# Idle matmuls on the outputs' bank, bias rows loaded by threes, and more rounds of the order planner, in an attention and channel-mix kernel

## The chip, the cores and the metric

The kernel runs on one core of a Trainium2 chip. The metric is the device time of one execution in microseconds, and the time given for a kernel is the median of its runs.

The engines are named as the profile names them: PE multiplies matrices (PEld is its weight load, which runs beside the matmuls), DVE, ACT and POOL work element by element, and SP issues all DMAs of this kernel, from one queue and in order.

## The reference

There are 8 batches, 8 heads, 576 positions and a head dimension of 64. The model width is 512 and the hidden width 1024.

```python
scores = scale * q @ k.T                              # per batch and head
cum = np.cumsum(np.maximum(s, 0.0), axis=-1)
bias = -(cum[:, :, :, None] - cum[:, :, None, :])
scores = np.where(causal, -1e9, scores + np.minimum(bias, 0.0))
attn = softmax(scores)
x = concat_heads(attn @ v)                            # [batch, position, 512]

xk = mu_k * x + (1 - mu_k) * x_prev                   # x_prev: one position earlier
xr = mu_r * x + (1 - mu_r) * x_prev
k = np.maximum(xk @ w_k, 0.0)
v = k * k @ w_v
out = sigmoid(xr @ w_r) * v
```

The matrices of the second part (w_k, w_r, w_v) arrive as 64-bit floats.

## The kernel before, in words

**Attention.** Heads are visited in pairs. The first batch is visited twice: first the early tiles (queries and keys 0 to 319, called A) of its four pairs, then the late ones (Z). The other batches are visited once, with all 576 positions. For each head `scores` makes the products into a PSUM bank "s" (there are two; L687 in the first visits, L698 afterwards). DVE reads them (L715), adds the bias row or the masked bias, keeps the running minimum nm and writes W. ACT makes the exponentials (L733) and POOL divides by the sums (L749). In `weighted` PE turns the weights over (L795), ACT and DVE copy them (L822, L857), PE multiplies them with the values into the one bank "po" (L913 in the first visits, L927 afterwards), and ACT copies that out (L948, L955). POOL makes the masked bias from the bias row with a select (L669). The bias row of a head, 128 copies of its cumulative sums, is loaded from cum_d in DRAM (L650) into one of two buffers "cb"; heads 0 and 1 of the first batch compute theirs (L475). cum_d itself is written once at the start (L457).

**Channel mix.** The results of a pair go to DRAM (L1277) and come back by chunks of 256 positions (L1178). There are 18 chunks. Each mixes neighbouring positions (ACT L1025, then DVE L1032), splits the result in two parts (L1054, L1058), and multiplies with w_k (L1086), w_r (L1128) and w_v (L1153) in three products each. Every block of a weight is loaded (L504), turned from 64-bit to two 32-bit parts by one ACT (L527), four DVE (L532 to L550), one ACT (L556) and one POOL instruction (L558), and stays in SBUF. The space of w_v blocks 4 to 7 holds the first batch's early results until those blocks are loaded.

**The order.** Nothing is issued in the order of the code. Every instruction is a task with an engine, a planned duration, the tasks it depends on and a due time. `Plan.forward` runs a list schedule over the engines with planned costs (TAIL and GAPS are what a result needs to reach another engine). `Plan.backward` makes new due times from that schedule. `Plan.run` does PASSES rounds of both and emits the order with the shortest planned time. While PE has nothing ready within 170 ns and the first split products (L698) have not been reached, `forward` puts in idle matmuls: 192 columns of an identity, planned at 82 ns each, which compute nothing that is used. They are not tasks, so the planner sees no dependence between them and others; the framework that emits the instructions adds semaphores by the tiles they touch.

The idle matmuls of the kernel before write columns 320 to 511 of one of the two "s" banks:

```python
idle = bank(1, "s", 2)
plan.idle = lambda: nc.tensor.matmul(
    idle.get()[:, 320:512], ...
```

Of the kernel before, what the change touches and what calls it, by code (L numbers as in the profile page):

```python
# [14 lines left out]
BF16 = mybir.dt.bfloat16  # L15
# [38 lines left out]
class Plan:  # L54
# [225 lines left out]
        return [-x for x in at]  # L280


    PASSES = 8

    def run(self):
        best = None
# [14 lines left out]
def forgetting_attention_then_channel_mix(  # L301
# [15 lines left out]
    nc = tc.nc  # L317

    B, H, D, S = q.shape
    DM, DF = moe_w_k.shape  # L320
    P = 128
# [16 lines left out]
    plan = Plan()  # L338

    def sbuf(shape, tag, bufs=1, dtype=F32):  # L340
        return plan.buffer(sb, shape, dtype, tag, bufs)

    def bank(n, tag, bufs=1):
        return plan.buffer(psum, [P, 512 * n], F32, tag, bufs)
# [28 lines left out]
    def dma(emit, reads, writes, ns):  # L373
        return plan.add("SP", max(500, 1.2 * ns), emit, reads, writes, land=1500)


    ident = fixed(const.tile([P, P], F32, name="ident"))
    make_identity(nc, ident.ap)


    idle = bank(1, "s", 2)
    plan.idle = lambda: nc.tensor.matmul(  # L382
        idle.get()[:, 320:512],
        ident.ap.bitcast(BF16)[:, 0:P],
        ident.ap.bitcast(BF16)[:, 0:192],
        start=True,
        stop=True,
    )
    QS = [0] + [64 + P * t for t in range(NQ - 1)]
    QN = [64] + [P] * (NQ - 1)  # L390
    KN = [QS[t] + QN[t] for t in range(NQ)]
# [40 lines left out]
    cum_d = fixed(dram.tile([B * H, S], F32, name="cum_d"))  # L432
# [132 lines left out]
    ALL, A, Z = tuple(range(NQ)), (0, 1, 2), (3, 4)  # L565
    first = []
# [78 lines left out]
    def scores(b, h, tiles, G, KH, KL):  # L645

        NK = KN[tiles[-1]]
        CB = sbuf([P, NK], "cb", 2) if not first else first.pop(0)
        (b == 0 and h < 2 and tiles == A) or dma(
            lambda: nc.sync.dma_start(  # L650
                CB.get(), cum_d.ap[b * H + h : b * H + h + 1, 0:NK].broadcast_to([P, NK])
            ),
            [cum_d], [CB], 819 * NK / S,
        )
        nm, sums, rinv = (sbuf([P, n], x, 2) for x, n in (("nm", 3 * NQ), ("sums", NQ), ("rinv", NQ)))
        if 0 in tiles:
            pool(lambda: nc.gpsimd.memset(sums.get()[:, 0:1], 1.0), [], [(sums, 0)], 1, 160)
        pt = early[h % 4] if tiles == A else weights[h % 2]


        M = sbuf([P, S], "mask", 2)

        def mask(m, k0, n):
            def own(x):
                x = x.get()[:m, k0 : k0 + n * m]
                return x if n == 1 else x.rearrange("p (t x) -> p t x", x=m)

            pool(
                lambda: nc.gpsimd.affine_select(  # L669
                    out=own(M),  # L670
                    in_=own(CB),
                    pattern=[[-1, m]] if n == 1 else [[0, n], [-1, m]],
                    base=0,
                    channel_multiplier=1,
                    compare_op=ALU.is_ge,
                    fill=MASK * ISCALE,
                ),
                [CB], [(M, k0 > 0)], n * m, 137,
            )

        def products(t, m, i, k0, w, W):
            ps = bank(1, "s", 2)
            q0 = QS[t] - QS[tiles[0]]
            if KL is None:
                r = slice(64 * (h % 2), 64 * (h % 2) + 64)
                pe(
                    lambda: nc.tensor.matmul(  # L687
                        ps.get()[:m, :w],
                        G.get()[r, q0 : q0 + m],
                        KH.get()[r, k0 : k0 + w],  # L690
                        start=True,
                        stop=True,
                    ),
                    [(G, x) for x in range(2)] + [(KH, x) for x in range(2)], [ps], w + 80, m, 4 / 2.4, 64,
                )
            for x, K in enumerate((KH, KL) if KL is not None else ()):
                y = pe(
                    lambda x=x, K=K: nc.tensor.matmul(  # L698
                        ps.get()[:m, :w],
                        G.get()[:, q0 : q0 + m],  # L700
                        K.get()[:, k0 : k0 + w],
                        start=x == 0,
                        stop=x == 1,
                    ),
                    [(G, x) for x in range(2)] + [(K, x) for x in range(2)], [ps], w, m,
                )
                if plan.busy_from is None:
                    plan.busy_from = y

            for a, e in ((k0, min(k0 + w, QS[t])), (max(k0, QS[t]), k0 + w)):  # L710
                if a >= e:
                    continue
                bias = CB if a < QS[t] else M
                dve(
                    lambda a=a, e=e, bias=bias, i=i: nc.vector.tensor_tensor_reduce(  # L715
                        out=W.ap[:m, a:e],
                        in0=ps.get()[:m, a - k0 : e - k0],
                        in1=bias.get()[:m, a:e],
                        scale=-SCALE,
                        scalar=3.0e38 if i == 0 else nm.get()[:m, 3 * t + i - 1 : 3 * t + i],  # L720
                        op0=ALU.add,
                        op1=ALU.min,
                        accum_out=nm.get()[:m, 3 * t + i : 3 * t + i + 1],
                    ),
                    [ps, (bias, 0 if bias is CB else t > 0)] + ([(nm, (t, i - 1))] if i else []),
                    [(W, i), (nm, (t, i))], e - a, extra=143 if i else 78,
                )
                i += 1
            return i

        def exponents(t, m, n, mi, W):
            act(
                lambda: nc.scalar.activation(  # L733
                    W.ap[:m, :n],
                    W.ap[:m, :n],
                    AF.Exp,
                    bias=nm.get()[:m, 3 * t + mi : 3 * t + mi + 1],
                    scale=-1.0,
                    accum_out=sums.get()[:m, t : t + 1],
                ),  # L740
                [(nm, (t, mi))], [(W, i) for i in range(3)] + [(sums, t)], n, 290, 1,
            )

        def normalize(t, m, n, W):


            to, c = (pt[1], P) if t == 0 else (W, 0)
            pool(
                lambda: nc.gpsimd.tensor_scalar(  # L749
                    out=to.ap[:m, c : c + n],  # L750
                    in0=W.ap[:m, :n],
                    scalar1=rinv.get()[:m, t : t + 1],
                    scalar2=1.0,
                    op0=ALU.mult,
                    op1=ALU.mult,
                ),
                [rinv] + [(W, i) for i in range(3)], [(to, i) for i in range(3)], n, 244,
            )

        def rs(x):  # L760
            return x.get()[:, tiles[0] : tiles[-1] + 1]

        if 0 in tiles:
            mask(64, 0, 1)
        mask(P, QS[max(1, tiles[0])], len([t for t in tiles if t]))
        for t in tiles:
            m, n, W = QN[t], KN[t], pt[t]
            i = 0
            for k0, w in [(0, n)] if n <= 512 else [(0, n // 2), (n // 2, n // 2)]:
                i = products(t, m, i, k0, w, W)  # L770
            exponents(t, m, n, i - 1, W)
        pool(
            lambda: nc.gpsimd.tensor_scalar(
                out=rs(rinv), in0=rs(sums), scalar1=1.0e-9, scalar2=None, op0=ALU.add
            ),
            [(sums, t) for t in tiles], [rinv], len(tiles), 310,
        )
        dve(lambda: nc.vector.reciprocal(rs(rinv), rs(rinv)), [], [rinv], 8 * len(tiles))  # L778
        for t in sorted(tiles, key=lambda t: (t == 0, t)):
            normalize(t, QN[t], KN[t], pt[t])  # L780
        return pt
# [202 lines left out]
    def channel_mix(ch, start, span, after):  # L984
# [3 lines left out]
        t = t0  # L988
# [16 lines left out]
        def mixed(which, c, xm):  # L1005
# [24 lines left out]
            for z in todo:  # L1030
                dve(
                    lambda z=z: nc.vector.scalar_tensor_tensor(  # L1032
                        out=to(*z),
                        in0=source(0, *z),
                        scalar=mu1.ap[:, which, c + z[0] : c + z[0] + 1],
                        in1=to(*z),
                        op0=ALU.mult,
                        op1=ALU.add,
                    ),
                    parts(*z[:2]) + [mu1] + [(xm, ("a", *u)) for u in todo],  # L1040
                    [(xm, ("d", *z))], z[2], extra=250,
                )

        def splits(c, xm, hi, lo):
# [188 lines left out]
    plan.due = -2.0e5  # L1233
    first.extend(first_sums(KN[A[-1]]))
    prefix_sums()
    QKs, Vs, early_x = {}, {}, []

    def load(n):
# [116 lines left out]
```

## Time and profile before

| what | value |
|---|---|
| median of three runs | 881.01 us (877.92 to 881.34) |
| the profiled execution, its time | 878.81 us |
| its span, first to last instruction | 877.0 us |
| mean granted clock of PE | 0.999 |
| busy in the span: PE, PEld, DVE, ACT, POOL | 857.3, 753.0, 672.2, 675.7, 493.0 us |

A busy PE is not a PE at its peak, since matmuls overlap; the busy time of its weight loads shows how densely they follow each other. Idle time of an engine is put down to what ended it. A wait for several events goes to the one that came last.

### The profile page before, as it was taken

How to read it: one execution, taken by the hardware profiler on the slowest of the kernel's cores; microseconds unless marked ns; L12 is line 12 of the kernel's file. 1: busy time of each engine (PE TensorE's matmuls, PEld its weight loads, DVE VectorE, ACT ScalarE, POOL GpSimd, SP SyncE). 2: the span in 40 equal slices, each digit the busy share in tenths (PEclk: the TensorE clock that was granted, in tenths of full speed). 3: DMA queues.
4: the chain of work that ended last, by engine and by line, in shares of the span. 5: the costliest groups of instructions: out<-in, count | busy, mean ns of one | idle time of the engine just before them, and what ended most of it. 6: DMA issues, size and time to landing. Idle time of an engine off the chain costs nothing. (4 is left out here: it accounts for less than half of the span.)

```text
span 877.0 us, 18381 instructions
## 1 busy us (share of the span) xinstructions
PE 857.3 (98%) x5591; PEld 753.0 (86%) x5591; DVE 672.2 (77%) x2385; ACT 675.7 (77%) x1810; POOL 493.0 (56%) x852
## 2 busy tenths in 40 slices
PE   8989999999999999999999999999999999999998
PEld 6669788888889898989898988898998989888996
DVE  6898878979887998789888787787786888655531
ACT  4898989989878898789878786878796878444331
POOL 4887989897665666566666466456646651100000
PEclk9999999999999999999999999999999999999999
DMA  7878854565454344334343436243525220201100
GB/s 239 240 215 243 240 169 136 176 158 164 122 147 116 124 137 128 99 124 138 118 147 111 126 102 159 65 135 111 158 84 145 84 70 34 62 14 36 49 25 25
DMA packets 63108, 109.05 MB, mean 124 GB/s; under 512 B 10144, under 2 KB 24480, under 8 KB 63008
## 3 DMA queue, kind: packets, MB, share of 16 engines
q1 hardware_dynamic: 63008, 107.87, 41.7%
q8 instruction: 44, 0.72, 0.3%
q14 instruction: 56, 0.46, 0.2%
HBM read 88.80 MB, written 19.04 MB: 123 GB/s over the span
## 5 line engine op out<-in xcount | busy, mean ns | idle before, releaser
L733 ACT ACTIVATE W<-W,nm 128x448 f32<-128x448 f32 (+4 forms) x320 | 179.8, 563 | 36.3 <-DVE nm L715 33.4
L1086 PE MATMUL m<-xh,w_k 128*128 128x256 f32 x976 | 204.4, 287 | 0.4 <-DVE kl L1115 0.2
L1153 PE MATMUL m<-w_v,kh 128*128 128x512 f32 x528 | 186.8, 404 | 0.0
L749 POOL TENSOR_SCALAR W<-W,rinv 128x192 f32<-128x192 f32 (+4 forms) x320 | 165.1, 534 | 17.3 <-DVE rinv L778 13.3
L795 PE MATMUL t<-ident,W 128*128 128x128 f32 (+1 forms) x896 | 164.1, 275 | 3.6 <-ACT ph L822 1.0
L1086 PEld LDWEIGHTS m<-xh,w_k 128*128 128x128 f32 x976 | 160.0, 189 | 3.2 <-DVE kl L1115 0.6
L1086 PE MATMUL m<-xl,w_k 128*128 128x256 f32 x488 | 140.2, 287 | 0.2 <-DVE xl L1058 0.2
L627 POOL TENSOR_TENSOR KL<-raw,KH 128x576 fp32r<-128x576 f32 x64 | 91.6, 1431 | 76.7 <-ACT KH L623 75.3
L795 PEld LDWEIGHTS t<-ident,W 128*128 128x128 f32 (+1 forms) x896 | 106.9, 132 | 26.1 <-DVE pl L826 2.5
L826 DVE TENSOR_TENSOR pl<-t,ph 128x512 fp32r<-128x512 f32 x224 | 107.8, 485 | 25.8 <-ACT ph L822 24.2
L698 PE MATMUL s<-KH,G 128*64 128x64 f32 (+3 forms) x360 | 110.4, 312 | 1.6 <-DVE nm L715 1.5
L822 ACT CAST ph<-t 128x512 fp32r<-128x512 f32 x224 | 93.2, 423 | 23.4 <-PE t L795 22.0
L1153 PEld LDWEIGHTS m<-w_v,kh 128*128 128x128 f32 x528 | 97.6, 189 | 13.9
L698 PE MATMUL s<-KL,G 128*64 128x64 f32 (+2 forms) x360 | 107.4, 301 | 0.0
L715 DVE CUSTOM_DVE_ANT_0 W<-s,cb 128x64 f32<-128x64 f32 (+3 forms) x256 | 94.7, 376 | 16.2 <-PE s L698 11.8
L1153 PE MATMUL m<-w_v,kl 128*128 128x512 f32 x264 | 105.6, 400 | 0.0
L638 POOL TENSOR_TENSOR G<-raw,G 64x576 fp32r<-64x576 f32 (+1 forms) x64 | 86.1, 1345 | 21.1 <-issue 7.6
L1025 ACT ACTIVATE xp<-x,mu 128x256 f32<-128x256 f32 (+3 forms) x184 | 77.6, 422 | 25.6 <-DMA x<-x_d 14.9
L1128 PE MATMUL m<-w_r,xh 128*128 128x512 f32 x264 | 95.0, 406 | 0.1
L1032 DVE SCALAR_TENSOR_TENSOR xp<-x,mu,xp 128x256 f32<-128x256 f32 (+3 forms) x184 | 76.5, 416 | 24.1 <-ACT xp L1025 21.8
L1086 PEld LDWEIGHTS m<-xl,w_k 128*128 128x128 f32 x488 | 92.2, 189 | 1.3 <-DVE xl L1058 0.4
L715 DVE CUSTOM_DVE_ANT_0 W<-s,mask,nm 128x128 f32<-128x128 f32 x256 | 86.9, 344 | 5.8 <-PE s L382 2.8
(146 smaller groups left out, 1903.4 us busy)
## 6 DMA issues: line engine op xcount, KB each, us to landing
raw<-in_k SPq DMA_DIRECT2D x128, 144.0 KB, 3.4
cb<-cum_d SPq DMA_DIRECT2D x64, 288.0 KB, 3.9
raw<-in_q SPq DMA_DIRECT2D x112, 144.0 KB, 3.5
out<-g SPq DMA_DIRECT2D x36, 256.0 KB, 2.3
vn<-in_v SPq DMA_DIRECT2D x28, 320.0 KB, 3.4
x_d<-xT SPq DMA_DIRECT2D x28, 288.5 KB, 2.4
x<-x_d SPq DMA_DIRECT2D x11, 514.0 KB, 4.3
w_k<-in_moe_w_k SPq DMA_DIRECT2D x8, 512.0 KB, 5.3
```

The lines of the kernel that those rows point to most:

```text
L627: lambda k=k, kh=kh, kl=kl: nc.gpsimd.tensor_tensor(out=kl.get(), in0=k.get(), in1=f32(kh.get()), op=ALU.subtract),
L638: lambda q=q, g=g: nc.gpsimd.tensor_tensor(out=g.get()[64:P], in0=q.get()[64:P], in1=f32(g.get()[64:P]), op=ALU.subtract),
L698: lambda x=x, K=K: nc.tensor.matmul(ps.get()[:m, :w], G.get()[:, q0 : q0 + m], K.get()[:, k0 : k0 + w], start=x == 0, stop=x == 1,),
L715: lambda a=a, e=e, bias=bias, i=i: nc.vector.tensor_tensor_reduce(out=W.ap[:m, a:e], in0=ps.get()[:m, a - k0 : e - k0], in1=bias.get()[:m, ...
L733: lambda: nc.scalar.activation(W.ap[:m, :n], W.ap[:m, :n], AF.Exp, bias=nm.get()[:m, 3 * t + mi : 3 * t + mi + 1], scale=-1.0, accum_out=s ...
L749: lambda: nc.gpsimd.tensor_scalar(out=to.ap[:m, c : c + n], in0=W.ap[:m, :n], scalar1=rinv.get()[:m, t : t + 1], scalar2=1.0, op0=ALU.mult ...
L795: lambda: nc.tensor.transpose(ps.get()[0:m, place : place + P], pt[t].ap[:, k0 : k0 + m], ident.ap),
L822: act(lambda: nc.scalar.copy(strips(ph), src()), [ps], [(ph, k) for k in ks], n * m)
L826: lambda: nc.vector.tensor_tensor(out=strips(pl), in0=src(), in1=f32(strips(ph)), op=ALU.subtract),
L1086: lambda u=u, f=f, c=c, n=n, w=w, x=x: nc.tensor.matmul(ps.get()[:, u * CT : (u + 1) * CT], weight["k", c, f // 4].get()[:, w, f % 4 * P : ...
L1128: lambda c=c, n=n, x=x, w=w: nc.tensor.matmul(ps.get(), x.get()[:, c, ts], weight["r", c, 0].get()[:, w], start=c == 0 and n == 0, stop=c ...
L1153: lambda f=f, n=n, x=x, w=w: nc.tensor.matmul(ps.get(), x.get()[:, f, ts], weight["v", f, 0].get()[:, w], start=f == 0 and n == 0, stop=f ...
```

## The change

The idle matmuls go to the bank "po". Only the first of them has the start flag, so that later ones do not clear a sum that is being built in other columns of the bank. The bias rows of heads 2 to 7 of the first batch, early tiles, are no longer loaded one by one into the two "cb" buffers but by threes into the space of w_v blocks 0 and 1. The planner does 48 rounds instead of 8. And the planned cost of the last DVE instruction of a mix is 130 ns plus its columns, where it was 250.

```diff
--- before.py
+++ after.py
@@ -280,7 +280,7 @@
         return [-x for x in at]
 
 
-    PASSES = 8
+    PASSES = 48
 
     def run(self):
         best = None
@@ -378,14 +378,21 @@
     make_identity(nc, ident.ap)
 
 
-    idle = bank(1, "s", 2)
-    plan.idle = lambda: nc.tensor.matmul(
-        idle.get()[:, 320:512],
-        ident.ap.bitcast(BF16)[:, 0:P],
-        ident.ap.bitcast(BF16)[:, 0:192],
-        start=True,
-        stop=True,
-    )
+    idle = bank(1, "po", 1)
+    idles = []
+
+    def one_idle():
+        idles.append(None)
+        nc.tensor.matmul(
+            idle.get()[:, 320:512],
+            ident.ap.bitcast(BF16)[:, 0:P],
+            ident.ap.bitcast(BF16)[:, 0:192],
+            start=len(idles) == 1,
+            stop=True,
+            skip_group_check=True,
+        )
+
+    plan.idle = one_idle
     QS = [0] + [64 + P * t for t in range(NQ - 1)]
     QN = [64] + [P] * (NQ - 1)
     KN = [QS[t] + QN[t] for t in range(NQ)]
@@ -645,13 +652,23 @@
     def scores(b, h, tiles, G, KH, KL):
 
         NK = KN[tiles[-1]]
-        CB = sbuf([P, NK], "cb", 2) if not first else first.pop(0)
-        (b == 0 and h < 2 and tiles == A) or dma(
-            lambda: nc.sync.dma_start(
-                CB.get(), cum_d.ap[b * H + h : b * H + h + 1, 0:NK].broadcast_to([P, NK])
-            ),
-            [cum_d], [CB], 819 * NK / S,
-        )
+        if first:
+            CB, part = first.pop(0), 0
+            bias_row = CB.get
+        elif b == 0 and tiles == A:
+            CB, part = early_bias[(h - 2) // 3], (h - 2) % 3
+
+            def bias_row():
+                return CB.get()[:, part]
+        else:
+            CB, part = sbuf([P, NK], "cb", 2), 0
+            bias_row = CB.get
+            dma(
+                lambda: nc.sync.dma_start(
+                    CB.get(), cum_d.ap[b * H + h : b * H + h + 1, 0:NK].broadcast_to([P, NK])
+                ),
+                [cum_d], [CB], 819 * NK / S,
+            )
         nm, sums, rinv = (sbuf([P, n], x, 2) for x, n in (("nm", 3 * NQ), ("sums", NQ), ("rinv", NQ)))
         if 0 in tiles:
             pool(lambda: nc.gpsimd.memset(sums.get()[:, 0:1], 1.0), [], [(sums, 0)], 1, 160)
@@ -662,20 +679,20 @@
 
         def mask(m, k0, n):
             def own(x):
-                x = x.get()[:m, k0 : k0 + n * m]
+                x = x()[:m, k0 : k0 + n * m]
                 return x if n == 1 else x.rearrange("p (t x) -> p t x", x=m)
 
             pool(
                 lambda: nc.gpsimd.affine_select(
-                    out=own(M),
-                    in_=own(CB),
+                    out=own(M.get),
+                    in_=own(bias_row),
                     pattern=[[-1, m]] if n == 1 else [[0, n], [-1, m]],
                     base=0,
                     channel_multiplier=1,
                     compare_op=ALU.is_ge,
                     fill=MASK * ISCALE,
                 ),
-                [CB], [(M, k0 > 0)], n * m, 137,
+                [(CB, part)], [(M, k0 > 0)], n * m, 137,
             )
 
         def products(t, m, i, k0, w, W):
@@ -710,19 +727,20 @@
             for a, e in ((k0, min(k0 + w, QS[t])), (max(k0, QS[t]), k0 + w)):
                 if a >= e:
                     continue
-                bias = CB if a < QS[t] else M
+                own = a >= QS[t]
+                bias, row = (M, M.get) if own else (CB, bias_row)
                 dve(
-                    lambda a=a, e=e, bias=bias, i=i: nc.vector.tensor_tensor_reduce(
+                    lambda a=a, e=e, row=row, i=i: nc.vector.tensor_tensor_reduce(
                         out=W.ap[:m, a:e],
                         in0=ps.get()[:m, a - k0 : e - k0],
-                        in1=bias.get()[:m, a:e],
+                        in1=row()[:m, a:e],
                         scale=-SCALE,
                         scalar=3.0e38 if i == 0 else nm.get()[:m, 3 * t + i - 1 : 3 * t + i],
                         op0=ALU.add,
                         op1=ALU.min,
                         accum_out=nm.get()[:m, 3 * t + i : 3 * t + i + 1],
                     ),
-                    [ps, (bias, 0 if bias is CB else t > 0)] + ([(nm, (t, i - 1))] if i else []),
+                    [ps, (bias, t > 0 if own else part)] + ([(nm, (t, i - 1))] if i else []),
                     [(W, i), (nm, (t, i))], e - a, extra=143 if i else 78,
                 )
                 i += 1
@@ -1038,7 +1056,7 @@
                         op1=ALU.add,
                     ),
                     parts(*z[:2]) + [mu1] + [(xm, ("a", *u)) for u in todo],
-                    [(xm, ("d", *z))], z[2], extra=250,
+                    [(xm, ("d", *z))], z[2], extra=250 if z is not todo[-1] else 130,
                 )
 
         def splits(c, xm, hi, lo):
@@ -1233,6 +1251,17 @@
     plan.due = -2.0e5
     first.extend(first_sums(KN[A[-1]]))
     prefix_sums()
+    early_bias = [sbuf([P, 3, KN[A[-1]]], f"w_v_{i}_0") for i in range(2)]
+    for i, x in enumerate(early_bias):
+        dma(
+            lambda i=i, x=x: nc.sync.dma_start(
+                x.get(),
+                cum_d.ap[2 + 3 * i : 5 + 3 * i, 0 : KN[A[-1]]]
+                .rearrange("(o h) t -> o h t", o=1)
+                .broadcast_to([P, 3, KN[A[-1]]]),
+            ),
+            [cum_d], [(x, y) for y in range(3)], 819 * 3 * KN[A[-1]] / S,
+        )
     QKs, Vs, early_x = {}, {}, []
 
     def load(n):
```

## Rows read from the trace of the kernel before

**Rows 1.** Busy time of each engine by stretch of the span.
```profile
core 0: us, PE busy (x) PEld busy (x) DVE busy (x) ACT busy (x) POOL busy (x), PEclk, DMA share, GB/s
8.00:20.00 12.00, 10.29 (x86) 7.45 (x83) 10.27 (x35) 5.98 (x17) 5.40 (x12) 1.00 0.72 238
20.00:44.00 24.00, 22.73 (x133) 14.60 (x131) 21.49 (x90) 21.32 (x77) 20.55 (x47) 1.00 0.82 247
44.00:60.00 16.00, 12.05 (x63) 8.53 (x63) 15.84 (x45) 15.70 (x43) 14.02 (x22) 1.00 0.75 208
60.00:90.00 30.00, 30.00 (x203) 26.93 (x202) 24.44 (x71) 27.43 (x68) 23.98 (x31) 1.00 0.87 253
90.00:260.00 170.00, 164.63 (x1055) 140.80 (x1053) 144.53 (x579) 153.82 (x429) 140.43 (x231) 1.00 0.57 161
260.00:660.00 400.00, 399.31 (x2685) 360.35 (x2684) 325.61 (x1204) 331.04 (x894) 242.24 (x414) 1.00 0.41 121
660.00:680.00 20.00, 18.85 (x124) 16.16 (x123) 13.47 (x55) 13.91 (x39) 11.05 (x16) 1.00 0.55 152
```

**Rows 2.** The idle matmuls: count, min/median/max in ns, first and last start.
```profile
L382 PE MATMUL s<-ident x159: 242/246/368, 1.8 to 43.2; 128*128 128x192 bf16 x159
```

**Rows 3.** Waits from 8 to 46 us: us in total, times, longest.
```profile
DVE W L715 <- PE s L382: 3.6, 9, 0.6
...
ACT W L733 <- DVE nm L715: 3.1, 4, 1.6
PE s L382 <- DVE nm L715: 2.7, 6, 0.6
...
POOL mask L669 <- DMA cb<-cum_d: 1.1, 2, 0.9
...
DVE W L715 <- POOL mask L669: 0.3, 1, 0.3
```

**Rows 4.** Timeline from 42 to 43.6 us: start, us, instruction, idle before and releaser.
```profile
42.17 0.66 PE L913 MATMUL po<-ph,V 128*128 128x192 f32 x4
42.18 0.34 DVE L715 CUSTOM_DVE_ANT_0 W<-s,cb 128x192 f32<-128x192 f32 x1
...
42.73 0.17 DVE L778 RECIPROCAL rinv<-rinv 128x3 f32<-128x3 f32 x1
...
42.89 0.58 PE L382 MATMUL s<-ident 128*128 128x192 bf16 x5
...
43.09 0.42 ACT L948 COPY w_v<-po 64x320 f32<-64x320 f32 x1
...
43.51 0.35 DVE L715 CUSTOM_DVE_ANT_0 W<-s,mask,nm 128x128 f32<-128x128 f32 x1 [0.62 <-PE s L382]
```

**Rows 5.** Waits of SP's queue from 8 to 46 us.
```profile
SPq L650 <- DVE nm L715: 16.8, 7, 5.4
```

**Rows 6.** Timeline, some rows between 5 and 60 us.
```profile
5.43 0.48 SPq L457 DMA_DIRECT2D cum_d<-mask  x1
...
14.71 0.33 SPq L650 DMA_DIRECT2D cb<-cum_d  x1
...
19.87 0.23 POOL L669 TENSOR_SCALAR_AFFINE_SELECT mask<-cb 64x64 f32<-64x64 f32 x1
...
46.05 0.33 PE L913 MATMUL po<-ph,V 128*128 128x64 f32 x2
...
47.66 0.42 ACT L948 COPY w_v<-po 64x320 f32<-64x320 f32 x1
...
59.10 0.58 SPq L504 DMA_DIRECT2D w_v<-in_moe_w_v  x1
```

**Rows 7.** ACT's copies out of the outputs' bank before 60 us.
```profile
L948 ACT COPY w_v<-po x8: 419/423/436, 23.4 to 55.1; 64x320 f32<-64x320 f32 x8
```

**Rows 8.** DMA issues before 60 us: count, KB each, median us to landing.
```profile
w_k<-in_moe_w_k SPq DMA_DIRECT2D x8, 512.0 KB, 5.3
...
cum_d<-mask SPq DMA_DIRECT2D x1, 144.0 KB, 4.1
```

## The prediction

> **What bounds the kernel now.** First the table of stretches, for which engine is full where [rows 1]. Between 8 and 60 us PE is not the limit: its idle matmuls, which compute nothing, all run before 43.2 us [rows 2]. DVE is: busy 21.49 of 24 us from 20 to 44 and 15.84 of 16 from 44 to 60, with ACT beside it (21.32 and 15.70). From 60 to 90 PE is full. From 90 to 260 all four are nearly full, and the weight loads, which show PE's density better than its busy time, take 140.80 of 170 us (0.828). From 260 to 660 PE has no holes and the share is 360.35 of 400 (0.901). At 660 to 680 it falls to 0.808 once. So the kernel is a DVE-bound head, a mixed middle and a PE-bound rest. A microsecond that DVE gains before 60 us starts everything behind it earlier; one gained by POOL or the DMA queue counts only if DVE, ACT or PE was waiting for it.
>
> Second, the waits of the head [rows 3] for what DVE lacks. From 8 to 44 us it idles 36 - 10.27 - 21.49 = 4.24 us, and 3.6 us of that are nine waits of the score reader (L715) for an idle matmul (L382). Six times an idle matmul waited for the reader in its turn, 2.7 us. One case in order of time shows the mechanism [rows 4]: five idle matmuls from 42.89 us, DVE free since 42.90, and its next score read starts only at 43.51, when the last of them ends. The idle matmuls write columns 320 to 511 of a score bank and the head's scores lie in columns 0 to 319, so no data passes: reader and writer are ordered by the bank.
>
> Third, SP's queue [rows 5, 6]. The load of head 2's bias row stands in it until DVE has read head 0's (there are two buffers): it is issued at 14.71 us after the longest such stop, 5.4 us, so from about 9.3 us SP issued nothing, with loads of queries and of w_k behind it. From 8 to 46 us these stops are 16.8 us in seven. Yet few consumers feel them: POOL waited 1.1 us for bias rows and DVE 0.3 us for a mask [rows 3].
>
> **The change, part by part.** (1) *Idle matmuls to the outputs' bank.* It takes away the nine waits, 3.6 us of DVE's time; this is the upper bound of the gain. What comes in their place: the bank of outputs is written by L913 and read by ACT's L948, one copy of 0.42 us for each of eight heads, from 23.4 to 55.1 us [rows 7]. Spread evenly, one every 4.5 us, five of them come up to 43.2 us, where the idle matmuls stop; the copy at 43.09 is the last of these. In [rows 4] L913 ends at 42.83, the idle matmuls run 42.89 to 43.47, and the copy starts at 43.09, while they still run. In the new place the copy waits for those put ahead of it. The planner starts the copy TAIL plus gap, 165 + 40 = 205 ns, after the products; at its 82 ns a piece, three idle matmuls come first. At the trace's 0.58 / 5 = 0.116 us that is 0.35 us a copy. I let one of the five meet no idle matmul, since they run in patches, so 4 x 0.35 = 1.4 us of ACT. Behind the copy on ACT stand the exponentials and the casts of weight blocks. Idle matmuls after the copy wait for it, 0.42 us, and real products behind those with them; where a product is not yet due this costs nothing. Before the first copy nothing reads the new bank, so the waits before 23.4 us vanish without a price. Bounds: -3.6 us, and +2.2 if ACT is delayed at all five by a whole run of five with the copy behind it (5 x (0.58 + 0.58) = 5.8, less 3.6). I take 3.6 - 1.4 = **-2.2 us**, nearer the gain, because DVE was the fuller engine.
>
> The Trainium skill bears on this: "PSUM — Partial Sum Buffer", section on bank collisions, asks for PSUM to be guarded by bank and quadrant and not by address. [rows 4] agree, since disjoint columns waited. By that rule the new bank orders ACT against the idle matmuls in the same way, and the move would be an exchange; it is the slower rival below.
>
> (2) *Bias rows of heads 2 to 7.* Six issues of 160 KB become two of 480 KB; the bytes are the same, six issues of 0.33 us go and two come [rows 6]. They wait for the cumulative sums: written from 5.43 us, landed 4.1 us later, at 9.5 [rows 6, 8]. A load of 512 KB lands in 5.3 us at the median of the head [rows 8], so head 2's rows are there at about 9.5 + 0.4 + 5.3 = 15.2 us; its first mask starts at 19.87 [rows 6], which leaves 4.7 us of cover. The second load has more. SP's stop up to 14.71 shrinks to the wait for the sums, and the loads behind it go some 4 us earlier. The new order puts 960 KB into the first stretch, where the channels moved 238 GB/s from 8 to 20 us [rows 1]: 4 us of transfer in front of what stands behind. That is about what the earlier issue gives back, so no weight block arrives later than before. w_v's space is free in time: the last early head's last read of its bias row starts at 42.18 [rows 4], and the first w_v load was issued at 59.10 [rows 6]. Gain: at least nothing, at most the rest of DVE's idle time in the head, 4.24 - 3.6 = 0.6, plus POOL's 1.1, in all -1.7. Loss: 0.6 us if the two loads delay a block for which DVE has nothing else to do. I take **-0.5 us**: the 0.3 us that DVE waited for a mask, and a little for POOL.
>
> (3) *48 rounds, and a shorter planned cost for the last mix of a chunk.* No instruction is added or removed; the order of all of them is drawn anew, because (1) and (2) alter the tasks and because the planner keeps the best plan of 48 instead of 8. The planned cost of the last L1032 falls from 256/0.96 + 250 = 517 to 397 ns; this moves only the estimate, and I count nothing for it. What an order can still win after 60 us: visible PE holes are 5.37 us (90 to 260), 0.69 (260 to 660) and 1.15 (660 to 680). If the middle were as dense as the rest, it would be 170 x (1 - 0.828/0.901) = 13.8 us shorter: the upper bound. What it can lose: more places like 660 to 680, which lost 20 x (1 - 0.808/0.901) = 2.1 us. Two of these are +4.2. I take one such place saved, **-2.1 us**, as the plan with the shorter estimate should have fewer of them.
>
> **The sum** against the profiled execution's own 878.81 us (span 877.0): -2.2 - 0.5 - 2.1 = -4.8, so 874.0. This execution lies 2.2 us below the median of the three runs, 881.01; the same step from the median gives 876.2. I take 875.5 us, 0.6% below the median. A step of 0.5% (4.4 us) is about what a measurement of this kernel can tell from no change, and the three runs themselves span 3.4 us.
>
> **Rivals.** *The early gain is taken back* (0.36): the 2.7 us of (1) and (2) arrive, but the new order is no better or loses one place of 2.1 us: 878.3 to 881, no change by the measure. For it: ACT is full as well from 20 to 60 us, so DVE's gain may turn into waits for ACT. Against it: ACT itself waited for DVE's minima in the head, 3.1 us [rows 3].
>
> *The order is worth much more* (0.12): half of the 13.8 us of the middle comes back, 6.9 + 2.7, and the time is 871.4 from the median. For it: 90 to 260 us is the one long stretch below the density of the rest. Against it: there ACT is busy 153.82 of 170 us, so an order alone can't bring all of it.
>
> *The new bank holds PE up* (0.08, slower): an idle matmul behind an output product waits for ACT's copy, and PE's real products wait behind it. That ACT can be late is seen once: output products end at 46.05 + 0.33 = 46.38 us, and the copy starts at 47.66, 1.28 us later [rows 6]. If ACT comes to the copy 1.2 us late and takes 0.42, PE stands 1.6 us at each of five evictions, 8 us less the 3.6 saved: 885.4 from the median. It decides from about 0.7 us a place, where the gain is gone; at 1.6 us the time is up 0.5%. The rule of the Trainium skill named above makes the same of the move. Beside it *a worse order* has 0.06: three more places like 660 to 680 less the early gain, some +4.
>
> *The forecast* has 0.38. Faster by over 0.5% is 0.38 + 0.12 = 0.50, within 0.5% 0.36, slower 0.14. The forecast's own range is 870 to 877. For eight in ten, the range must reach past the larger gain and to the worse order: 866 (the 13.8 us and a little of the rest) to 883.5.
>
> **What the profile will show.** If (1) is right, no score reader waits for L382 before 44 us, DVE's idle time from 8 to 44 us falls from 4.24 to under 2, and ACT's copy out of the outputs' bank begins to wait for L382. If (2) is right, SP's hole after 9 us closes, and head 2's mask waits for no load. If (3) is right, the weight loads' share from 90 to 260 us rises above 0.828, or the stall near 670 is gone. The first full stretch of PE should begin 2 to 3 us before 60. The forecast is wrong if PE's first full stretch starts no earlier, if idle matmuls and copies wait for each other by over 3 us, or if the middle loses density through the new order.

## The result and the profile after

The changed kernel takes 867.63 us (median of four runs, 866.49 to 869.06), the kernel before 881.17 (median of four, 877.92 to 882.25): a ratio of 0.985 (0.982 to 0.988). By the ratio that is 13.0 us less, 1.5% (13.5 by the two medians). The forecast of 875.5 had the sign and missed the size: it promised 5.5 us, and 2.4 times as much came. The time also lies below the forecast's own range of 870 to 877. The profiled execution took 867.92 us (span 866.1, mean granted clock 0.998), 10.9 less than that of before.

The table of stretches of the kernel after, to be laid beside [rows 1] (same columns; the first line is a stretch that [rows 1] does not have):

```profile
0.00:60.00 60.00, 54.52 (x343) 40.74 (x344) 51.32 (x178) 47.93 (x144) 44.83 (x104) 0.97 0.78 249
8.00:20.00 12.00, 12.00 (x109) 9.46 (x106) 11.19 (x40) 6.95 (x22) 6.49 (x16) 1.00 0.96 331
20.00:44.00 24.00, 23.14 (x128) 14.98 (x125) 22.40 (x90) 22.47 (x79) 20.62 (x47) 1.00 0.76 230
44.00:60.00 16.00, 13.21 (x66) 10.40 (x67) 14.54 (x47) 15.86 (x43) 14.95 (x19) 0.89 0.74 226
60.00:90.00 30.00, 30.00 (x198) 26.63 (x197) 25.04 (x76) 28.11 (x69) 26.12 (x35) 1.00 0.81 234
90.00:260.00 170.00, 166.98 (x1119) 147.44 (x1118) 148.44 (x593) 157.79 (x442) 140.60 (x236) 1.00 0.57 164
260.00:660.00 400.00, 399.47 (x2668) 359.36 (x2667) 327.49 (x1211) 331.97 (x898) 244.64 (x412) 1.00 0.41 122
660.00:680.00 20.00, 20.00 (x163) 19.57 (x162) 15.41 (x60) 14.20 (x40) 12.32 (x24) 1.00 0.47 140
680.00:760.00 80.00, 79.52 (x520) 70.98 (x519) 57.24 (x190) 54.82 (x148) 24.04 (x46) 1.00 0.17 53
760.00:860.00 100.00, 100.00 (x582) 87.89 (x581) 44.56 (x78) 39.20 (x76) 0.00 (x0) 1.00 0.09 30
```

The same table of the kernel before, in three stretches that [rows 1] does not have:

```profile
0.00:60.00 60.00, 51.25 (x331) 36.61 (x332) 50.84 (x170) 45.65 (x138) 42.74 (x103) 1.00 0.77 231
...
680.00:760.00 80.00, 80.00 (x527) 71.99 (x526) 63.83 (x223) 60.44 (x164) 32.53 (x60) 1.00 0.20 62
760.00:860.00 100.00, 100.00 (x622) 89.61 (x621) 48.14 (x83) 42.68 (x83) 0.00 (x0) 1.00 0.10 33
```

Of the first 60 us the idle matmuls' own weight loads have to be taken off, 14.61 us before and 14.87 after (the same view, of their line alone). What is left is useful: 36.61 - 14.61 = 22.00 before, 40.74 - 14.87 = 25.87 after. So PE is ahead by 3.9 us of weight loads at 60 us. Not all of this is work. By number it has done 344 - 155 = 189 useful loads, where it had done 332 - 159 = 173; but the changed kernel has a stretch at a lower clock from 50 to 56 us (last section), where a load of w_k's products takes 330 ns against a mean of 189. A run without that stretch (e12, below) has done 188 loads by then in 23.68 us, so some 2 of the 3.9 us are longer loads. These are the idle matmuls of the kernel after:

```profile
L386 PE MATMUL po<-ident x155: 243/246/368, 1.8 to 35.1; 128*128 128x192 bf16 x155
```

PE gains 147.44 - 140.80 = 6.6 more from 90 to 260 us and 19.57 - 16.16 = 3.4 from 660 to 680, and is behind by 4.0 in the other four stretches together. Up to 860 us that is 9.9 us more, of which some 7.7 are work. At the 0.901 of [rows 1] it takes PE 8.5 us to do as much; the profiled executions differ by 10.9, and the rest is not placed by this table. The gain has two main places: the head, and the mixed middle, whose share of weight loads rose from 0.828 to 0.867. A part of the 3.4 near 670 us may be another mix of matmuls; what is sure is that PE's hole of 1.15 us there is gone (0.48 us of holes lie behind it now, from 680 to 760).

PE's first full stretch begins 1.9 us earlier. These are the last matmuls of the head with an idle time before them, first of the kernel before, then of the kernel after:

```profile
58.46 0.41 PE L795 MATMUL t<-ident,W 128*64 128x128 f32 x2 [0.71 <-ACT ph L822]
...
56.60 0.38 PE L1104 MATMUL m<-xl,w_k 128*128 128x256 f32 x1 [0.34 <-DVE xl L1076]
```

Next the waits of the changed kernel from 8 to 46 us, where [rows 3] stood before (L733 is the score reader, L966 the copy out of the outputs' bank, L386 the idle matmul):

```profile
DVE W L733 <- PE s L704: 1.2, 4, 0.4
...
PEld po L931 <- ACT w_v L966: 1.0, 3, 0.4
PEld L386 <- issue: 0.9, 3, 0.4
...
ACT w_v L966 <- PE po L386: 0.5, 2, 0.3
```

No score reader waits for an idle matmul any more, and the copy waits for them 0.5 us in two. DVE's idle time from 8 to 44 us is 36 - 11.19 - 22.40 = 2.41 us, where it was 4.24.

Last SP's queue. Its stops for bias rows, 16.8 us in seven before [rows 5], are now mainly the last two of these (up to 46 us; L667 the single rows, L1257 the loads by threes). But SP stops for loads of V instead (L579), 8.7 us in two:

```profile
SPq L579 <- PE po L931: 5.1, 1, 5.1
SPq L579 <- PE s L704: 3.6, 1, 3.6
...
SPq L667 <- DVE nm L733: 1.9, 1, 1.9
...
SPq L1257 <- DMA cum_d<-mask: 1.6, 1, 1.6
```

The timeline of SP's issues shows the hole after 9 us of [rows 6] closed, with both loads by threes and loads of V, queries and w_k in it:

```profile
9.41 0.38 SPq L1257 DMA_DIRECT2D w_v<-cum_d  x1
9.84 0.48 SPq L511 DMA_DIRECT2D w_k<-in_moe_w_k  x1
10.37 0.43 SPq L579 DMA_DIRECT2D V<-in_v  x1
10.84 0.43 SPq L605 DMA_DIRECT2D G<-in_q  x1
...
13.44 0.66 SPq L1257 DMA_DIRECT2D w_v<-cum_d  x1
```

And the masks of heads 2 to 7 (count; min/median/max in ns; first and last start):

```profile
L686 POOL TENSOR_SCALAR_AFFINE_SELECT mask<-w_v x12: 233/322/413, 15.6 to 33.7; 64x64 f32<-64x64 f32 x6, 128x256 f32<-128x256 f32 x6
```

Head 2's first mask starts at 15.6 us instead of 19.87 [rows 6].

### The profile page after: what moved, and what is told of

Read it like the earlier page. It is cut to its first block, busy times and chain, and to the rows that moved or that the text cites. A ratio compares the mean times of both kernels' runs of the same rounds, so it can differ in the third digit from the quotient of the medians.

```text
span 866.1 us, 18396 instructions
## 1 busy us (share of the span) xinstructions
PE 852.5 (98%) x5587; PEld 753.9 (87%) x5587; DVE 670.2 (77%) x2385; ACT 674.0 (78%) x1810; POOL 492.6 (57%) x852
## 4 chain that ended last, share of the span: by engine, by line
PE 92%; DMA 2%; ACT 2%; DVE 2%; issue 1%; POOL 0%; ACTq 0%; DVEq 0%; SPq 0%; POOLq 0%
PE m L1171 20%; PE m L1104 19%; PE t L813 11%; PE m L1146 11%; PE s L715 10%; PE po L945 9%; PE po L931 2%; DMA x<-x_d 2%; PE t L1171 2%; PE po L386 2%; PE s L1104 2%; PE t L1104 2%; PE s L704 1%; PE t L945 1%; PE po L1146 1%
## 5 line engine op out<-in xcount | busy, mean ns | idle before, releaser
L767 POOL TENSOR_SCALAR W<-W,rinv 128x192 f32<-128x192 f32 (+4 forms) x320 | 165.1, 535 | 13.4 <-DVE rinv L796 9.6
L844 DVE TENSOR_TENSOR pl<-t,ph 128x512 fp32r<-128x512 f32 x224 | 107.1, 486 | 21.7 <-ACT ph L840 19.9
L733 DVE CUSTOM_DVE_ANT_0 W<-s,cb 128x64 f32<-128x64 f32 (+2 forms) x244 | 91.0, 380 | 17.7 <-PE s L715 13.2
L1146 PE MATMUL m<-w_r,xh 128*128 128x512 f32 x264 | 92.1, 403 | 0.0
L945 PE MATMUL po<-ph,V 128*128 128x448 f32 x280 | 89.4, 320 | 0.5 <-ACT ph L840 0.5
```

The costliest lines, as they stand in the source:

```text
L733: lambda a=a, e=e, row=row, i=i: nc.vector.tensor_tensor_reduce(out=W.ap[:m, a:e], in0=ps.get()[:m, a - k0 : e - k0], in1=row()[:m, a:e], ...
L767: lambda: nc.gpsimd.tensor_scalar(out=to.ap[:m, c : c + n], in0=W.ap[:m, :n], scalar1=rinv.get()[:m, t : t + 1], scalar2=1.0, op0=ALU.mult ...
L844: lambda: nc.vector.tensor_tensor(out=strips(pl), in0=src(), in1=f32(strips(ph)), op=ALU.subtract),
L945: lambda: nc.tensor.matmul(po.get()[: P if both else 64, at + q0 - base : at + q0 - base + m], V.get()[:, kb, 2 * j : 2 * j + (2 if both e ...
L1146: lambda c=c, n=n, x=x, w=w: nc.tensor.matmul(ps.get(), x.get()[:, c, ts], weight["r", c, 0].get()[:, w], start=c == 0 and n == 0, stop=c ...
```

## The experiments

The theory after the result: the bank is worth what was predicted, and the rest is the order. 48 rounds find a better one, and the bias rows help by letting the planner move heads, not by saving waits. The rivals: the rows save the time by themselves (fewer issues, or no buffer waits), or the gain is one lucky draw of the planner (a draw is the one order that a setting of the planner happens to give). No kernel below leaves out work. Each was timed beside the kernel before, whose medians were 880.0 to 881.1 us in the five sets; ratios are to it, with 95% intervals.

**One part alone.** e1 is the kernel before with the new `one_idle`, in an unchanged order:

```diff
-    idle = bank(1, "s", 2)
+    idle = bank(1, "po", 1)
...
+            start=len(idles) == 1,
```

> The kernel before with nothing changed but the bank of the idle matmuls; every engine's instructions keep the order of before. Theory A (the waits of the score reader for idle matmuls were worth their 3.6 us less what ACT's copies now wait): 2 to 3 us faster than before, 878 to 879 where before has 881, and DVE's idle time from 8 to 44 us falls from 4.24 to about 2. Theory B (the new order alone carries the gain): within 1 us of before, since what DVE gains it loses to the next instruction in an order made for other waits. Slower by 2 us or more would mean that the copies hold PE up.

878.62 us, ratio 0.998 (0.996 to 0.9995): 1.8 us by the ratio, with an interval of 0.4 to 3.2, and 2.5 by the medians. DVE's nine waits are gone, and ACT's copy (L955 here) waits instead, 1.8 us in three where 1.4 were predicted. Who waited for the idle matmuls in e1, and what DVE waited for from 8 to 44 us:

```profile
ACT w_v L955: 1.8, 3
...
DVE W L722 <- PE s L694: 1.7, 4, 0.9
DVE m L539 <- ACT m L534: 1.5, 1, 1.5
```

The term of -2.2 holds in size. Its making holds in part: DVE is busy 10.41 us from 8 to 20 and 22.06 from 20 to 44, so its idle time fell from 4.24 only to 3.53 us, where about 2 was expected. Most of what it saved it now waits for real products and for ACT.

e2 has 48 rounds and nothing else; e6 has 13:

```diff
-    PASSES = 8
+    PASSES = 48
```

> The kernel before with 48 rounds instead of 8 and nothing else. The planner's own estimate falls from 861.15 to 858.80 us. Theory B (the order carries the gain): 8 us or more faster, 873 or less. Theory A with bias rows (the head's waits carry it): 1 to 3 us faster, as the estimate says, 878 to 880.

> The kernel before with 13 rounds; the planner's estimate is 860.21 us, 0.94 below that of 8 rounds. Theory C (the order that 8 rounds chose was a poor draw: its stall near 670 us and its thin middle are its own): 871 to 875, with no dip of the weight loads at 660 to 680. Theory D (the time follows the planner's estimate): 880 to 881.

e2: 873.24 us, 0.9915 (0.989 to 0.994). e6: 874.04, 0.992 (0.990 to 0.994). The planner's own estimates are 861.15 us for 8 rounds, 860.21 for 13 and 858.80 for 48; an estimate lower by 0.94 us came with 7 us on the chip. The stretches of e2, columns as in [rows 1]:

```profile
90.00:260.00 170.00, 168.06 (x1113) 147.25 (x1112) 148.81 (x599) 158.83 (x443) 139.24 (x233) 1.00 0.58 165
660.00:680.00 20.00, 20.00 (x143) 18.36 (x142) 15.56 (x54) 15.14 (x39) 11.07 (x16) 1.00 0.56 166
```

Nearly the whole +6.6 of the middle is here (147.25 against 140.80), by the order alone, with ACT busy 158.83 of 170 us. The head is not: its useful weight loads are 22.27 us up to 60, against 22.00.

e3 is the changed kernel with 8 rounds, e4 the changed kernel with the idle matmuls back on the score bank.

> The changed kernel with 8 rounds instead of 48: new bank, bias rows by threes, new planned cost. The planner's estimate is 861.09 us, that of before to 0.1 us. Theory A (the head's waits and the bias loads carry it): 6 us or more faster than before, 875 or less. Theory B (48 rounds carry it): at most 3 us faster, 878 or more.

> The changed kernel with the idle matmuls back on the score bank; the order of all instructions is that of the changed kernel. Theory A: the waits of the score reader for idle matmuls come back and cost 2 to 4 us against the changed kernel's 867.6, so 870 to 872. Theory B: within 1 us of 867.6.

e3: 871.41 us, 0.990 (0.987 to 0.992), so the rounds are worth 3.8 us here, not 7.5. e4: 868.62, 0.987 (0.985 to 0.990): the bank 1.0 us here. The parts don't add up to the whole, one by one.

e7 has only the shorter planned cost, e8 this and 48 rounds:

```diff
-                    [(xm, ("d", *z))], z[2], extra=250,
+                    [(xm, ("d", *z))], z[2], extra=250 if z is not todo[-1] else 130,
```

> The kernel before with the new planned cost of the last mix alone and 8 rounds; the planner's estimate is 865.24 us, 4.1 above before. Theory C (before is a poor draw): no slower than before in spite of the estimate, 874 to 881. Theory D (the time follows the estimate): 884 to 886.

> The kernel before with the new planned cost and 48 rounds, without new bank and without new loads of bias rows; the estimate is 856.96 us, 0.3 below that of the changed kernel. If the order alone makes the whole gain: 867 to 869.5, as the changed kernel. If the loads by threes are worth 3 us or more beside it, since the head's loads no longer wait: 871 or more.

e7: 879.18 us, 0.9985 (0.997 to 0.9998), with an estimate of 865.24, 4.1 above that of before. e8: 874.49, 0.994 (0.992 to 0.996), with 856.96, the second lowest estimate of all. Over a few microseconds the estimate does not rank kernels.

**The bias rows with the order held.** e5 is e1 with heads 2 to 7's rows still loaded one by one, in the old order, but into places of their own:

```diff
+        own_place = b == 0 and h > 1 and tiles == A
...
+        if own_place:
+            CB.get = lambda: row_place((h - 2) // 3)[:, (h - 2) % 3]
```

> The kernel before in its old order, with the new bank for the idle matmuls, and with a place of their own for the early bias rows of heads 2 to 7 (in the space of w_v blocks 0 and 1, still six loads in their old places of SP's queue), so that no such load waits for a buffer. Both direct effects of the change without a new order. If the rows' buffers held the head up, 2 us or more below the run with the new bank alone (878.6), so 876.6 or less; if POOL and DVE were hardly waiting for rows, within 1 us of it, and SP's stop before 14.7 us is gone all the same.

878.38 us, 0.9988 (0.997 to 1.000), against e1's 878.62. SP's hole is closed, as its issues show:

```profile
10.05 0.33 SPq L671 DMA_DIRECT2D w_v<-cum_d  x1
10.43 0.45 SPq L605 DMA_DIRECT2D G<-in_q  x1
```

Yet it brought nothing clear: 0.2 us less than e1 by the medians, 0.7 more by the ratios. So the rows' buffer waits cost nothing in the old order. SP stops no less for that; it goes on to the next loads of V and stands there, 11.6 us in three:

```profile
SPq L579 <- PE t L816: 9.5, 2, 4.9
SPq L579 <- PE po L934: 2.1, 1, 2.1
```

e10 is the changed kernel with six loads of one row in place of two of three, into the same places.

> The changed kernel with the two loads of three rows cut into six loads of one row each, in the same place and known to the planner; 48 rounds, new bank, new cost; the estimate is 858.32 us. If the place is what counts: within 2 us of the changed kernel, 866.5 to 869.5. If fewer and larger loads count: 870 or more.

867.29 us, 0.985 (0.983 to 0.987): fewer, larger loads are worth nothing either, as far as one more draw of the order can show it. What is left is the place, and an order that uses it.

**The bias rows with the order free.** e9 is the kernel before with the rows by threes, e11 this with 48 rounds, both with the old bank and cost; e14 and e13 are e9 and e11 with the new bank, their orders untouched.

> The kernel before with the bias rows by threes alone: old bank, old planned cost, 8 rounds. The planner's estimate is 860.36 us, 0.8 below before. Theory E (rows that are there early let the order draw the head's scores forward, 3 us or more whatever the draw): 870 to 873.5, and by 60 us PE has done 23.8 us or more of useful weight loads, where before has 22.0. Theory C (only the draw matters): 873 to 880, with 22 to 23 us of loads.

> The kernel before with the bias rows by threes and 48 rounds: old bank, old planned cost; the estimate is 857.69 us. Theory E and C together (draw some 7, rows some 4): 867.5 to 870.5. Theory C alone: 872.5 to 875, as the two runs of 48 rounds without the rows.

> The order of the run with bias rows by threes and 48 rounds, instruction for instruction, with the idle matmuls moved to the outputs' bank (this is the changed kernel with the old planned cost). Theory F (on the score bank the idle matmuls of this order wait for DVE, PE stands still for part of the time near 18 to 21 us, its clock falls to half and the head is drawn out in about half of the executions; the new bank takes these waits away): no execution with the half clock before 45 us, all of them at 866.5 to 869.5, spread under 3 us where the score bank gave 869 to 881. Against F: the spread stays, with a median of 870 to 873.

> The order of the run with bias rows by threes and 8 rounds, instruction for instruction, with the idle matmuls on the outputs' bank. Theory F: the clock stays full from 20 to 40 us, and the time falls from 877.7 to 871 to 874, that is by more than twice the 1.8 us that the bank gave in the old order. Against F: 875.5 to 877.

e9: 877.66 us, 0.9975 (0.995 to 0.9998). e11: 872.95, 0.9935 (0.990 to 0.997). e14: 872.50, 0.992 (0.990 to 0.994). e13: 867.99, 0.986 (0.983 to 0.988). The bank, which was worth 2 us before, is worth 5 here. e9 has a mean clock of 0.984 to 0.994 in ten of its eleven executions. Six of e11's executions took 869.0 to 873.0 us with a mean clock of 0.995 to 0.998 and five 880.1 to 881.4 with 0.982 or 0.983; the six alone (middle 870.5) leave the bank 2.5 us, and the rest goes with a stretch at the lower clock. It lies in e11's profiled execution like this (columns as in [rows 1]):

```profile
16.00:22.00 6.00, 4.77 (x35) 3.41 (x34) 3.72 (x18) 2.66 (x8) 4.30 (x12) 0.86 1.05 399
22.00:44.00 22.00, 21.57 (x63) 12.91 (x64) 12.97 (x53) 12.66 (x44) 11.39 (x28) 0.50 0.42 115
```

and in that of e13, same order, new bank:

```profile
16.00:22.00 6.00, 6.00 (x38) 3.69 (x36) 5.96 (x29) 5.07 (x19) 5.67 (x16) 1.00 0.98 372
22.00:44.00 22.00, 20.46 (x111) 13.12 (x109) 20.07 (x79) 20.95 (x73) 19.48 (x41) 1.00 0.86 244
```

In the waits of e11 from 8 to 22 us, idle matmuls and score readers (L726) stop each other:

```profile
DVE W L726 <- PE s L382: 2.3, 5, 0.9
...
PE s L382 <- DVE nm L726: 1.9, 5, 0.5
```

PE stands for 1.23 of 6 us there, its granted clock falls to 0.50, which is the 1.2 GHz level, and up to 44 us everything that hangs on PE goes slowly: DVE is busy 12.97 of 22 us, where e13, with the clock at 1.00 in both stretches, has 20.07. Since the bank is all that differs, and the fall came in five of eleven executions against none of five, the old bank is what lets the clock fall in this order. Why it falls here is open: the kernel before has 2.7 us of such stops of PE [rows 3] and keeps 1.00.

e16 is e2 with the new bank, e17 is e8 with it, that is, the changed kernel without the bias rows.

> The kernel before with 48 rounds and the new bank, without the bias rows by threes and with the old planned cost; the order is that of the run with 48 rounds alone (873.2). If the rows are worth 3 us or more beside the rounds and the bank: 871 to 873, and at most 23 us of useful weight loads by 60 us. If the draw and the bank together make the whole gain: 867 to 869.

> The same with the new planned cost, so the changed kernel without the bias rows by threes; the order is that of the run with 48 rounds and the new cost (874.5), the estimate 856.96 us is 0.3 below the changed kernel's. If the rows are worth 3 us or more: 871 to 874. If not: 867 to 869.

e17: 871.90 us, 0.9905 (0.988 to 0.993); the rows are worth 4.3 us. e16: 875.62, 0.993 (0.991 to 0.996), no faster than e2 and in neither of the ranges expected for it. Its executions run from 869.9 us (mean clock 1.0) to 877.4 (0.994); the three with 0.998 and more have 871.6 in the middle, 1.6 under e2, all of whose executions had 0.999 or 1.0. So in this order it is the new bank that goes with a lower clock; where e16 loses it no trace shows, since the profiled execution had 0.999.

e17's profile shows what the rows do when the order is free. Its stops of SP for bias rows up to 46 us:

```profile
SPq L657 <- DVE nm L722: 16.2, 8, 4.9
```

and its stretches, columns as in [rows 1]:

```profile
0.00:60.00 60.00, 52.60 (x340) 38.90 (x341) 52.70 (x176) 45.65 (x140) 42.40 (x103) 1.00 0.78 232
90.00:260.00 170.00, 165.50 (x1086) 144.02 (x1086) 147.73 (x589) 155.90 (x435) 139.21 (x231) 1.00 0.59 164
```

Beside the same stretches of the changed kernel: by 60 us ACT has done 2.3 us more and POOL 2.4 more when the rows have places of their own, DVE 1.4 less. PE has done 189 useful weight loads against 341 - 154 = 187, so it is hardly ahead there (the busy times, 25.87 against 24.13 us, differ by the changed kernel's longer loads). In the middle it is: 147.44 us against 144.02, 1118 loads against 1086. Where the heads stand is read from head 2's first mask in e17, and from ACT's eight copies out of the outputs' bank, first of e17, then of the changed kernel:

```profile
18.30 0.59 POOL L676 TENSOR_SCALAR_AFFINE_SELECT mask<-cb 64x64 f32<-64x64 f32 x2
...
L955 ACT COPY w_v<-po x8: 404/422/426, 21.6 to 53.9; 64x320 f32<-64x320 f32 x8
...
L966 ACT COPY w_v<-po x8: 415/422/423, 24.0 to 52.0; 64x320 f32<-64x320 f32 x8
```

The mask starts at 15.6 us in the changed kernel, 2.7 earlier, and the last copy 1.9 earlier.

**Beyond the change.** e15 has 103 rounds (and the old cost), e12 lets the idle matmuls go on until the first product of the channel mix:

```diff
-                if plan.busy_from is None:
-                    plan.busy_from = y
...
+                        if plan.busy_from is None:
+                            plan.busy_from = y
```

> The changed kernel with the old planned cost and 103 rounds; the planner's estimate is 856.62 us, 0.7 below the changed kernel. Theory D (time follows the estimate): 866 to 867. If estimates closer than 2 us say nothing about the time: anywhere from 866 to 871.

> The changed kernel, but idle matmuls go on until the first product of the channel mix instead of the first split product of the scores; 48 rounds, estimate 857.09 us. If the half clock that the changed kernel shows from about 51 to 55 us costs time: no stretch below full clock and 865 to 866.6. If PE has slack there: 867 to 869.

e15: 868.48 us, 0.9865 (0.984 to 0.989), with an estimate of 856.62, the lowest of all and under the 857.29 of the changed kernel. e12: 866.80, 0.9845 (0.983 to 0.987), between the two ranges expected for it. Neither is told apart from the changed kernel.

All medians together, in us; each column is one of rows and bank, each line a number of rounds and a cost:

| | neither | bank | rows | both |
|---|---|---|---|---|
| 8 rounds, old cost | 881.1 | 878.6 (e1) | 877.7 (e9) | 872.5 (e14) |
| 8 rounds, new cost | 879.2 (e7) | | | 871.4 (e3) |
| 48 rounds, old cost | 873.2 (e2) | 875.6 (e16) | 873.0 (e11) | 868.0 (e13) |
| 48 rounds, new cost | 874.5 (e8) | 871.9 (e17) | 868.6 (e4) | 867.6 |

Each part can be read from six pairs that differ in it alone. Bank: +2.4 to -5.2, mean -2.3. Rows: -0.3 to -7.6, mean -4.6. Rounds: -3.0 to -7.9, mean -4.8. Cost: +1.3 to -4.3, mean -1.7. The means add up to -13.4, close to the whole, but the spread of each shows how much one pair says. A bank pair has one order; in the other pairs each kernel is a draw of its own. Against the rival of one lucky draw: all seven kernels with rows and bank (e10, e12 and e15 among them) take 866.8 to 872.5 us, all five with neither (e6 among them) 873.2 to 881.1.

## Why the prediction was off, point by point

- **The bank, -2.2: right** in size (-1.8 in e1, a mean of -2.3), and in the mechanism as far as the nine waits go; that DVE would wait for other things in their place was left out (3.53 us idle in e1). The loss bound of +2.2 has a slip: the copy behind a run of idle matmuls is 0.42 us and not 0.58, so it is 5 x 1.00 - 3.6 = +1.4. The rule of the Trainium skill ("PSUM — Partial Sum Buffer", on bank collisions) is borne out: in e1 ACT's copy waits for idle matmuls in columns that it doesn't read. The move was still no even exchange, since 1.8 us of ACT's waits came for 3.6 of DVE's. What the term left out is PE's clock: on the score bank it falls in e9 and e11, and in e16 it is lower on the new bank.
- **The bias rows, -0.5: this step failed.** "Gain: at least nothing, at most ... -1.7" was worked out from the waits in the order of before, and with that order nothing clear came (e5 against e1). But the order is drawn anew. In six pairs the rows bring 4.6 us on average, 4.1 more than forecast, and beside the rest of the change they bring 4.3 us (e17 against the changed kernel), or 3.4 between the executions of both with a mean clock of 0.998 and more (870.8 and 867.4, three each). The likely way: the buffers are a constraint on the order that no consumer's wait shows. With only two, head 2's load can't go before head 0's last read, so the planner has laid the heads out that far apart, and consumers wait little; with the constraint gone the heads move. This is read from e5, e10 and e17 together, from the masks' start (15.6 us, 18.3 in e17, 19.9 before) and from the last copy (52.0, 53.9, 55.1); no run moved the heads alone, and more than half of the 4.3 us is not seen there.
- **The order, -2.1: this step failed too, in size.** It was sized as "one such place" like the stall at 670 us; 48 rounds alone bring 7.5 us (e2), 4.8 on average. That place did go, and beside it the middle gained 6.6 us of weight loads, which at 0.901 take PE 7.4 us, about half of the upper bound of 13.8. The rival *the order is worth much more* said 6.9; it had 0.12, and against it stood "there ACT is busy 153.82 of 170 us". As a reason against half of the bound that was a misreading: ACT had 16 us to spare, and took up 4 (157.79), as e2 did by the order alone (158.83). This rival's 871.4 is still 3.8 us too high, since it left the rows at their small price.
- **The cost, nothing: not settled.** It alters no instruction, yet each pair is a new draw of the order, from +1.3 to -4.3 us.
- **The signs to look for** came in the main: no score reader waits for the idle matmul, SP's hole closed, head 2's mask waits for no load, the middle rose above 0.828, the stall near 670 went. PE's first full stretch moved by 1.9 us, from 58.46 to 56.60, where 2 to 3 before 60 was said. DVE's idle time stayed at 2.41 where "under 2" was said.

Not settled: why the order of 8 rounds is so much poorer than its estimate, how much of the rows' worth depends on which order it meets, and what makes PE's clock fall in one order on one bank.

## What to carry to other kernels

A planned order hides its constraints: a buffer count that no consumer waits for can still cost microseconds, so try a relaxed resource with the order held and with it free. Where the order is searched, time several draws, because a planner's estimate that moves by 1 us can go with 7 us on the chip. An engine at 90% is not a wall; ask what the share could still become.

## What was not expected of the hardware

The idle matmuls do not keep PE's clock up in every order and on every bank: on the score bank the order of e11 gave 0.50 for 22 us in the execution shown, and with the new bank the same order had 1.00 from 16 to 44 us. In the changed kernel itself a dip is left, after the idle matmuls end (last start 35.1 us). Its stretches, columns as in [rows 1]:

```profile
50.00:52.00 2.00, 1.59 (x8) 1.22 (x7) 2.00 (x8) 1.98 (x5) 1.56 (x2) 0.79 0.89 243
52.00:54.00 2.00, 2.00 (x10) 1.96 (x10) 1.90 (x5) 1.97 (x5) 1.82 (x4) 0.50 0.60 193
54.00:56.00 2.00, 1.59 (x11) 1.19 (x9) 1.50 (x5) 1.98 (x6) 2.00 (x4) 0.86 0.89 278
```

The same in e12, whose idle matmuls go on, and below it the first 60 us of e12 and of its idle matmuls alone (41.83 - 18.15 = 23.68 us of useful loads, 377 - 189 = 188 of them):

```profile
50.00:52.00 2.00, 2.00 (x22) 1.98 (x22) 1.97 (x8) 1.56 (x5) 1.78 (x3) 1.00 0.40 126
52.00:54.00 2.00, 1.78 (x17) 1.46 (x16) 1.57 (x3) 1.95 (x5) 1.92 (x2) 1.00 0.61 137
54.00:56.00 2.00, 1.31 (x9) 1.12 (x10) 1.20 (x5) 1.97 (x7) 1.12 (x3) 1.00 0.76 192
...
0.00:60.00 60.00, 55.53 (x376) 41.83 (x377) 50.12 (x173) 46.41 (x142) 44.06 (x105) 1.00 0.81 249
...
0.00:60.00 60.00, 22.05 (x189) 18.15 (x189) 1.00 0.81 249
```

The clock stays at its upper level, and 866.80 us against 867.63 is all that came of it, which is not told apart. e12 runs another order, so the dip's own price is not shown.
